# The opening of a fused state-space and feed-forward kernel: C over two queues, decay differences in other banks, the first top words copied by GpSimd

## The chip, the cores and the metric

The kernel runs on one core of one Trainium2 chip. The metric is the device time of one execution in microseconds; the median of the runs of a kernel counts. Each core has a matrix engine (TensorE, PE), a vector engine (VectorE, DVE), a scalar engine (ScalarE, ACT), GpSimd (POOL) and SyncE (SP), which here only issues transfers. Transfers can be issued from SP and from ACT; both share the core's 16 DMA engines.

## What is computed

Shapes: 4 batches, 8 heads, 768 tokens, head size 32, state size 16; feed-forward 256 to 2048 to 256.

```python
log_a = np.log(np.clip(a, 1e-06, 1.0))
for each chunk of 32 tokens:
    cum = np.cumsum(la, axis=-1)
    L = np.exp(cum[:, :, :, None] - cum[:, :, None, :]) * causal
    CB = np.einsum('bhin,bhjn->bhij', Cc, Bc)
    y_intra = np.einsum('bhij,bhjd->bhid', CB * L, xc)
    y_inter = np.einsum('bhin,bhnd->bhid', Cc, state) * np.exp(cum)[..., None]
    y[:, :, sl] = y_intra + y_inter
    state = exp(sum(la)) * state + sum_j(Bc x xc * exp(cum[-1] - cum_j))
# then, with the heads side by side (3072 tokens of 256):
h = x @ w_in
out = (h * np.clip(h + 3.0, 0.0, 6.0) / 6.0) @ w_out
```

The two weight matrices are given as 64-bit floats.

## The kernel before

The 768 tokens are worked in six chunks of 128 for all four batches at once, each as two halves of 64. The order of instructions on each engine is that of the program; nothing is rescheduled.

For a chunk, `diff_mask`, `diff_less` and `diff_pick` build the differences of the summed logarithms in PSUM (chunks 0 and 1), `diff_exp` takes their exponential into `L` on ScalarE, `scores` multiplies C with B (`cb`) and brings x into the state (`into_state`), `multiply` forms `L` times `cb` on VectorE, `mix` forms y (with `from_state`), and `keep` copies y into `yT`, the input of the feed-forward part. For chunk 0 `turn_squares` transposes C on VectorE and `part_heads` spreads it into `cT`; `turn_b` transposes B on TensorE; `first_eto` and `fade` scale C by the decay; `ends` scales B by the decay (`bs`, on GpSimd).

The feed-forward part of chunk 0 runs over f = 0 to 15, blocks of 128 hidden units: `mlp_in` makes two matmuls of 128x512 into one of four PSUM banks (f modulo 4), `ramp` (ScalarE) and `times_ramp` (VectorE) turn them into `gT`. Behind it `first_out` multiplies with `w_out` in four groups. Later chunks use products with fewer multiplications (`lead`, `early`, `middle`, `last`, `out_units`).

The weights come as eight parts of 1 MB (`raw`, three buffers): parts 0 to 3 are quarters of `w_in`, 4 to 7 of `w_out`. `decode(i)` is a generator that turns a part from 64-bit words into 32-bit floats in steps: a copy of the top 16 bits (`ws`, ScalarE), the masks of exponent and sign (VectorE), the upper and the lower words of the significand (`wm`, VectorE), two ScalarE steps on the exponent (`we`), and sign and product (VectorE). `weights(i, n)` takes n steps. In the loop over f, the table `weave` takes one step of parts 2 to 5 at each f.

Transfers, in the program's order: `a` on SP; the first weights and B of chunk 0 on ACT; C of chunk 0 in eight pieces (`pairs_first`), x and the second weights on SP. Every transfer uses one of eight completion slots in turn, and an issue waits until the previous transfer on its slot is complete. The PSUM banks are called f0 to f3, two called o, and y0 and y1. The order of the opening is written out at the end of the program, from `diff_mask` to `load(1)`.

Of the kernel before, what the change touches and what calls it, by code (L numbers as in the profile page):

```python
# [20 lines left out]
def kernel(  # L21
# [63 lines left out]
    def load_bc(c):  # L85
# [10 lines left out]
        def pairs_first(src):  # L96
            t = loads.tile([P, 2, NB, 4, N], FP32, name="pairs", tag="bc")
            for b in range(NB):
                for h in range(2):
                    nc.sync.dma_start(  # L100
                        out=t[:, h, b].rearrange("s a n -> s (a n)"),
                        in_=src[b, h:NH:2, sl, :].rearrange("h (s a) n -> h s (a n)", a=4))
            return t
# [3 lines left out]
        Bs[c] = tokens_first(B, nc.scalar if c == 0 else nc.sync, name="B")  # L107
        if c == 0:
            bcs[c] = [pairs_first(C), Bs[c]]
        elif c < TURN:  # L110
# [17 lines left out]
    def load_w(i, queue=nc.sync):  # L128
# [10 lines left out]
        queue.dma_start(out=dst, in_=src)  # L139
        raws[i] = raw  # L140

    load_w(0, nc.scalar)
    load_bc(0)
    load_x(0)
    load_w(1)
    nc.scalar.preload_act_table_set("natural_log_exp_and_others")
# [40 lines left out]
    def decode(i):  # L187
# [10 lines left out]
        nc.scalar.copy(out=s, in_=top)  # L198

        def significand():  # L200
# [3 lines left out]
            yield  # L204
            nc.vector.scalar_tensor_tensor(
                out=m.bitcast(FP32), in0=lo, scalar=2.0 ** -32, in1=m, op0=ALU.mult,
                op1=ALU.add)
            yield

        parts_m = significand()  # L210
        if i == 0:
            next(parts_m)
            next(parts_m)
        yield
        nc.vector.tensor_scalar(
            out=e, in0=s, scalar1=0x7FF0, scalar2=None, op0=ALU.bitwise_and)
        nc.vector.tensor_scalar(
            out=s, in0=s, scalar1=0x8000, scalar2=None, op0=ALU.bitwise_and)
        next(parts_m, None)
        yield  # L220
        nc.scalar.activation(e.bitcast(BF16), e, AF.Relu, bias=bias_hi, scale=-8.0)
        yield
        nc.scalar.activation(e, e.bitcast(BF16), AF.Relu, bias=bias_lo, scale=-1.0)
        next(parts_m, None)
        if i and i + NRAW < 2 * NP:
            load_w(i + NRAW)
        yield
        nc.vector.tensor_tensor(out=e, in0=e, in1=s, op=ALU.bitwise_or)
        m, e = m.bitcast(FP32), e.bitcast(BF16)
        if i < NP:  # L230
            dst = w_in[:, :, i * FP * P:(i + 1) * FP * P]
# [345 lines left out]
    def mix(c):  # L577
# [5 lines left out]
        for u in range(2):  # L583
# [8 lines left out]
            if c == 0:  # L592
                from_state(c, 1, (2 * u, 2 * u + 1))
# [441 lines left out]
```

## Time and profile before

| | us |
|---|---|
| median of three runs | 360.6 (359.11 to 360.76) |
| the profiled execution, time | 359.64 |
| the profiled execution, span | 357.9 |
| PE busy | 347.9 (97%), 3936 instructions |
| DVE busy | 221.9 (62%), 426 |
| ACT busy | 177.5 (50%), 390 |
| POOL busy | 137.9 (39%), 139 |
| DMA | 24.97 MB in 75482 packets |

A profile shows one execution. Its span runs from the first to the last instruction; the execution's own time lies 1.74 us above it. Busy times are averages over stages with different limits, so that a stage is read from the chain of waits (the work that ended last, followed back) and from the timeline of each engine. "Idle before" names what released an engine. A matmul of 128x512 in 32-bit floats has two records.

### The profile page before, as it was taken

The page shows a single profiled execution, that of the slowest core. Times are in us where ns is not written, and L with a number is a line of the kernel's source. Part 1 is how long each engine was busy: PE and PEld are TensorE (multiplying, and loading weights), DVE is VectorE, ACT ScalarE, POOL GpSimd, SP SyncE. Part 2 cuts the span into 40 slices and gives each one's busy share as a digit, 9 for nine tenths or more (in the row PEclk, how much of TensorE's full clock was granted, in tenths as well). Part 3 has the DMA queues.
Part 4 walks back from the last instruction along what each step waited for, and adds up shares of the span by engine and source line. Part 5 has one row for each costly group of instructions (what it writes and reads, how often), then busy time and mean ns, then how long its engine had stood idle before and what let it go on. Part 6 is the DMA issues. An engine that isn't in the chain of part 4 may idle for free.

```text
span 357.9 us, 9350 instructions
## 1 busy us (share of the span) xinstructions
PE 347.9 (97%) x3936; PEld 300.0 (84%) x3936; DVE 221.9 (62%) x426; ACT 177.5 (50%) x390; POOL 137.9 (39%) x139
## 2 busy tenths in 40 slices
PE   5799999999999999999999999999999999999996
PEld 2554458888888999888999888999888999888996
DVE  6599999975887463686444687434587431588111
ACT  4678887267763730674650575560576010476100
POOL 3300000362599521099522089610068600058700
PEclk9899999999999999999999999999999999999999
DMA  8979969502924061550043560001000000000000
GB/s 166 201 277 185 266 165 127 116 4 84 155 57 60 5 136 58 81 80 2 4 113 82 74 88 2 4 2 35 26 2 1 4 3 31 29 3 0 2 29 31
DMA packets 75482, 24.97 MB, mean 70 GB/s; under 512 B 66032, under 2 KB 71824, under 8 KB 74928
## 3 DMA queue, kind: packets, MB, share of 16 engines
q1 hardware_dynamic: 71056, 23.06, 33.9%
q10 hardware_dynamic: 4384, 1.31, 1.7%
q8 instruction: 31, 0.51, 0.6%
q14 instruction: 11, 0.09, 0.1%
HBM read 21.07 MB, written 3.29 MB: 68 GB/s over the span
## 4 chain that ended last, share of the span: by engine, by line
PE 91%; DVE 3%; DMA 3%; ACT 1%; SPq 1%; issue 0%; DVEq 0%; ACTq 0%
PE ob L766 18%; PE even L652 18%; PE oa L766 18%; PE odd L652 13%; PE o L707 8%; PE h L610 8%; PE y L588 3%; PE y L500 2%; PE cb L522 2%; DMA raw<-in_moe_w_in_dram 2%; DMA pairs<-in_C_dram 1%; PE y L534 1%; SPq L100 1%; DVE odd L681 0%; DVE up L668 0%
## 5 line engine op out<-in xcount | busy, mean ns | idle before, releaser
L752 POOL TENSOR_TENSOR s<-gT 128x512 f32<-128x512 f32 x20 | 26.4, 1318 | 89.7 <-DVE gT L693 89.7
L652 PE MATMUL even<-ts,w_sum 128*128 128x256 f32 x160 | 48.2, 383 | 0.0
L667 ACT COPY even<-odd 128x512 f32<-128x512 f32 x40 | 23.0, 576 | 48.6 <-PE odd L652 46.3
L688 ACT ACTIVATE gT<-odd,half 128x512 f32<-128x512 f32 x40 | 27.5, 688 | 34.9 <-DVE odd L681 34.9
L652 PE MATMUL odd<-yT,w_in 128*128 128x256 f32 x160 | 41.1, 379 | 0.0
L766 PE MATMUL oa<-w_out,gT 128*128 128x128 f32 x320 | 38.9, 277 | 0.0
L766 PEld LDWEIGHTS oa<-w_out,gT 128*128 128x128 f32 x320 | 38.1, 192 | 0.9
L766 PE MATMUL ob<-w_out,s 128*128 128x128 f32 x320 | 37.4, 275 | 0.0
L766 PEld LDWEIGHTS ob<-w_out,s 128*128 128x128 f32 x320 | 36.5, 192 | 0.0
L652 PEld LDWEIGHTS even<-ts,w_sum 128*128 128x128 f32 x160 | 29.9, 190 | 5.3 <-ACT up L674 1.5
L693 DVE SCALAR_TENSOR_TENSOR gT<-gT,odd 128x512 f32<-128x512 f32 x40 | 27.5, 688 | 9.9 <-ACT gT L688 9.9
L652 PEld LDWEIGHTS odd<-yT,w_in 128*128 128x128 f32 x160 | 30.1, 190 | 3.9
L385 ACT ACTIVATE L<-L,cum_n 128x64 f32<-128x64 f32 x128 | 31.1, 339 | 0.0
L766 PE MATMUL ob<-t,gT 128*128 128x128 f32 x240 | 30.3, 279 | 0.0
L688 ACT ACTIVATE gT<-even,half 128x512 f32<-128x512 f32 x40 | 27.8, 695 | 4.4 <-PE even L652 4.4
L693 DVE SCALAR_TENSOR_TENSOR gT<-gT,even 128x512 f32<-128x512 f32 x40 | 27.2, 680 | 4.4 <-ACT gT L688 4.4
L766 PEld LDWEIGHTS ob<-t,gT 128*128 128x128 f32 x240 | 27.9, 192 | 1.2 <-issue 0.5
L707 PE MATMUL o<-w_out,gT 128*128 128x256 f32 x128 | 28.7, 381 | 0.0
L668 DVE COPY up<-odd 128x256 f32<-128x256 f32 x40 | 17.0, 424 | 18.6 <-ACT even L667 17.9
L610 PE MATMUL h<-yT,w_in 128*128 128x512 f32 x64 | 27.7, 594 | 0.0
L707 PEld LDWEIGHTS o<-w_out,gT 128*128 128x128 f32 x128 | 24.1, 190 | 3.7 <-issue 0.5
L563 DVE TENSOR_TENSOR L<-L,cb 128x512 f32<-128x512 f32 x24 | 15.3, 681 | 18.0 <-PE cb L522 15.5
(130 smaller groups left out, 609.8 us busy)
## 6 DMA issues: line engine op xcount, KB each, us to landing
raw<-in_moe_w_out_dram SPq DMA_DIRECT2D x4, 1024.0 KB
L<-cum_d SPq DMA_DIRECT2D x8, 512.0 KB
xt<-in_x_dram SPq DMA_DIRECT2D x6, 512.0 KB
raw<-in_moe_w_in_dram SPq DMA_DIRECT2D x3, 1024.0 KB
out_dram<-res SPq DMA_DIRECT2D x20, 128.0 KB
eto<-cum_e SPq DMA_DIRECT2D x20, 64.0 KB
B<-in_B_dram SPq DMA_DIRECT2D x5, 256.0 KB
raw<-in_moe_w_in_dram ACTq DMA_DIRECT2D x1, 1024.0 KB
```

Of the source, the lines that this page charges most:

```text
L385: nc.scalar.activation(Ls[c][:, b, h], Ls[c][:, b, h], AF.Exp, bias=cum_n[:, c, g:g + 1])
L563: nc.vector.tensor_tensor(out=Ls[c][:, :, hs], in0=Ls[c][:, :, hs], in1=cbs[c][q], op=ALU.mult)
L588: nc.tensor.matmul(out=ys[c][a, u][d0:d0 + D, b], lhsT=xt[rows, b * NH + h], rhs=Ls[c][rows, b, h], start=(b == 0 and a >= min(c, 1)), sto ...
L610: nc.tensor.matmul(out=h.rearrange("p r i -> p (r i)"), lhsT=w_in[:, j, f * P:(f + 1) * P], rhs=yTs[k][:, j].rearrange("p b i -> p (b i)") ...
L652: nc.tensor.matmul(out=bank[:, r], lhsT=lhsT, rhs=rhs, start=start, stop=True, skip_group_check=True)
L667: nc.scalar.copy(out=even, in_=odd[:, 1:2].to_broadcast([P, 2, 2 * P]))
L668: nc.vector.tensor_copy(out=up[:, 1], in_=odd[:, 0])
L688: nc.scalar.activation(gTs[k][:, f], h.rearrange("p r i -> p (r i)"), AF.Relu, bias=half, scale=1.0 / 6.0)
L693: nc.vector.scalar_tensor_tensor(out=g, in0=g, scalar=1.0, in1=h.rearrange("p r i -> p (r i)"), op0=ALU.min, op1=ALU.mult)
L707: nc.tensor.matmul(out=o[:, b % 2], lhsT=gTs[0][:, f, b * P:(b + 1) * P], rhs=w_out[:, f], start=(f == 0 and b % 2 == 0), stop=True, skip_ ...
L752: nc.gpsimd.tensor_tensor(out=o, in0=p_, in1=q_, op=op)
L766: nc.tensor.matmul(out=bank[:, slot], lhsT=lhs[:, j], rhs=rhs[:, j], start=(clear and j == 0), stop=True, skip_group_check=True)
```

## The change

C of chunk 0 is loaded in pieces of 32 partitions with all four batches, in place of 128 partitions and one batch, alternately from ACT and SP. The first weights move from ACT to SP, behind C; B follows them on SP, then x, and the second weights in four pieces. ScalarE's table load now stands ahead of its transfers.

The differences of chunk 0 use the banks o and y0, y1 in place of f0 to f3. Those of chunk 1 are split: the masks and `diff_less` of batches 0 and 1 stay in the opening, their `diff_pick` goes to f = 3, all of batches 2 and 3 to f = 5, and the exponentials of batches 2 and 3 into `first_out`.

For part 0 the top words are copied by GpSimd, and the lower words, sign and product stand behind the decay products. For part 1 all steps stand behind `keep`. The loads of parts 2 and 3, formerly issued ahead of and behind `scores`, are issued from ACT behind the first step of part 1 and from SP behind f = 0; `load_eto(1)` and `load(1)` go to f = 1. `turn_cum` moves into the middle of `mix(0)`, the filler matmul `busy` ahead of it is gone, and one copy of `in_three` goes to ScalarE.

```diff
-        def pairs_first(src):
+        def pairs_first(src, queues=(nc.sync, nc.sync)):
             t = loads.tile([P, 2, NB, 4, N], FP32, name="pairs", tag="bc")
-            for b in range(NB):
+            for q in range(NQ):
                 for h in range(2):
-                    nc.sync.dma_start(
-                        out=t[:, h, b].rearrange("s a n -> s (a n)"),
-                        in_=src[b, h:NH:2, sl, :].rearrange("h (s a) n -> h s (a n)", a=4))
+                    queues[h].dma_start(
+                        out=t[32 * q:32 * q + 32, h].rearrange("s b a n -> s b (a n)"),
+                        in_=src[:, 2 * q + h, sl, :].rearrange("b (s a) n -> s b (a n)", a=4))
...
-        Bs[c] = tokens_first(B, nc.scalar if c == 0 else nc.sync, name="B")
         if c == 0:
-            bcs[c] = [pairs_first(C), Bs[c]]
-        elif c < TURN:
+            bcs[c] = [pairs_first(C, (nc.scalar, nc.sync))]
+            load_w(0)
+        Bs[c] = tokens_first(B, name="B")
+        if c < TURN:
...
-        queue.dma_start(out=dst, in_=src)
+        for r in range(n):
+            rows = slice(r * P // n, (r + 1) * P // n)
+            queue.dma_start(out=dst[rows], in_=src[rows])
...
-    load_w(0, nc.scalar)
+    nc.scalar.preload_act_table_set("natural_log_exp_and_others")
     load_bc(0)
     load_x(0)
-    load_w(1)
-    nc.scalar.preload_act_table_set("natural_log_exp_and_others")
+    load_w(1, n=4)
...
+        def words():
+            if i == 0:
+                nc.gpsimd.tensor_copy(out=s, in_=top)
+            else:
+                nc.scalar.copy(out=s, in_=top)
...
+        def more():
+            if i + NRAW < 2 * NP:
+                load_w(i + NRAW)
...
+        order = {
+            0: ((words,), (upper,), (masks,), (above,), (below,), (lower,), (sign, product),
+                (more,)),
+            1: ((words,), (upper,), (masks, above), (lower, below), (sign, product), (more,)),
+        }.get(i, ((words,), (masks, upper), (above,), (below, lower, more), (sign, product)))
...
-        nc.vector.tensor_copy(part[G:2 * G], mid)
+        nc.scalar.copy(out=part[G:2 * G], in_=mid)
...
-        if c == 0:
-            d = ps.tile([P, NH, HT], FP32, name="d", tag=f"f{b}")
-        elif b < 2:
+        if b < 2:
...
-        take(c)
+        if c:
+            take(c)
...
+            if then is not None and u == 0:
+                then()
...
     diff(0, 0, 1)
     diff(0, 2, 3)
+    turn_squares(bcs[0][0], turned(0)[2])
+    part_heads(0)
     weights(0, 1)
+    weights(0, 1)
+    add_up(ends_at[1])
+    store_rows()
     for b in range(NB):
         diff_exp(0, b)
+        ends(0, b)
+    for b in range(2):
+        diff_mask(1, b)
+    turn_b(0)
     first_eto()
-    diff(1, 2, 3)
...
+    for b in range(2):
+        diff_less(1, b)
     fade(0, HALF[1], nc.gpsimd)
...
-    load_w(2)
+    weights(0, 2)
     weights(0, 1)
     scores(0)
     multiply(0)
-    load_w(3)
-    c_ps = ps.tile([P, NC, G], FP32, name="c_ps", tag="f1")
-    turn_cum(c_ps)
-    busy(1, ps.tile([P, NB * P], FP32, name="d", tag="f0"))
-    weights(0, 1)
+    weights(0, 2)
+    c_ps = ps.tile([P, NC, G], FP32, name="c_ps", tag="f2")
+    mix(0, lambda: turn_cum(c_ps))
+    by_token(c_ps)
+    keep(0)
     weights(1, 1)
-    by_token(c_ps)
-    mix(0)
-    keep(0)
-    weights(1, 3)
+    load_w(2, nc.scalar)
+    weights(1, 4)
     renew(0)
-    weights(1, 1)
-    load_eto(1)
-    load(1)
...
                 mlp_in(k, f)
+                if f == 0:
+                    weights(0, 1)
                 for i in weave.get(f, []):
                     weights(i, 1)
-                if f in (6, 8):
+                if f == 1:
+                    load_eto(c)
+                    load(c)
+                elif f == 2:
+                    weights(1, 1)
+                elif f == 3:
+                    for b in range(2):
+                        diff_pick(c, b)
+                elif f == 5:
+                    diff_two(c, 2, 3)
+                elif f in (6, 8):
                     diff_exp(c, f // 2 - 3)
...
+                    elif (i, b) in ((0, 1), (0, 2)):
+                        diff_exp(c, b + 1)
```

## The prediction

> **What bounds the kernel now.** I read the busy table of the page first (TensorE 97% of the span), then the chain of waits in order of time, because a busy share cannot say where an opening is bound.
>
> ```profile
> 0.80 5.83 DMA raw<-in_moe_w_in_dram
> 7.31 1.21 SPq L100
> 8.56 4.29 DMA pairs<-in_C_dram
> 13.03 1.10 DVE csT L465
> 15.19 2.12 PE cb L522 x64
> 17.31 1.30 DVE L L563 x2
> 19.08 1.05 PE d L490 x2
> ...
> 23.36 27.66 PE h L610 x64
> 51.02 15.54 PE o L707 x72
> ```
>
> Columns are start, length, what. Up to 23.3 us the chain is a chain of latencies. Transfers share eight completion slots; the sixth C transfer takes the slot of the first weights (`raw`), so SP waits until `raw` has landed (7.31), C is complete only at 12.85, and everything follows: transpose, `cb`, decay products, `mix`. From 23.3 us on TensorE never waits: 64 records of `h` at 0.433 each, then `o`. So the time is (start of the first `h`, called M, now 23.29) plus all TensorE work behind it plus its stalls. An instruction put behind M costs its full TensorE time, unless TensorE stands still there.
>
> Next the table by short stretches (length, busy time with counts of PE, PEld, DVE, ACT, POOL, then granted clock, DMA share, GB/s):
>
> ```profile
> 6.00:6.50 0.50, 0.00 (x0) 0.00 (x0) 0.47 (x2) 0.00 (x0) 0.00 (x0) 1.00 1.52 167
> 8.00:8.50 0.50, 0.50 (x33) 0.50 (x32) 0.47 (x2) 0.04 (x1) 0.00 (x0) 1.00 0.37 41
> 15.50:16.00 0.50, 0.50 (x32) 0.50 (x27) 0.50 (x1) 0.00 (x0) 0.50 (x1) 0.50 1.02 336
> 20.50:21.00 0.50, 0.50 (x54) 0.41 (x31) 0.50 (x1) 0.00 (x0) 0.00 (x0) 1.00 1.05 426
> ```
>
> The 64-byte pieces of B move at 167 GB/s, the late C pieces at 41, weights at about 400; and `cb` runs at clock 0.50. Last, the timeline of VectorE and ScalarE around M:
>
> ```profile
> 20.43 1.23 DVE L236 SCALAR_TENSOR_TENSOR w_in<-wm,we 128x1024 f32<-128x1024 f32 x1
> 26.48 1.13 ACT L198 COPY ws<-raw 128x1024 uint16<-128x1024 uint16 x1
> 26.77 1.23 DVE L236 SCALAR_TENSOR_TENSOR w_in<-wm,we 128x1024 f32<-128x1024 f32 x1
> 34.37 1.23 DVE L236 SCALAR_TENSOR_TENSOR w_in<-wm,we 128x1024 f32<-128x1024 f32 x1
> ```
>
> Quarter 0 of `w_in` is ready at 21.7, quarter 1 at 28.0 (needed at M + 6.9 = 30.2), quarter 2 at 35.6 (needed 37.2): the weight decoding runs only 1.6 us ahead.
>
> **Two rules of the Trainium skill.** "DMA: Bandwidth & Descriptors", in the section on why a DMA increments its semaphore by 16, says that a transfer from SP or ACT runs on the largest number of engines up to 16 that divides the slowest dimension of both sides. Old C transfers have 4 heads against 128 partitions, hence 4 engines; the DMA share of 0.37 at 41 GB/s while they were alone fits roughly. New ones have 32 and 32, hence 16. I go by it: C's eight pieces stop being slow. "TensorE: Matmul & The Clock Gate", Part 1, says that about 3.4 us of idleness halves the clock and as much work restores it. The trace halves it at about 15.1 after only 2.4 us without matmuls and restores it at about 18.4; I go by the trace, and keep `cb` at its half-speed 2.1 us.
>
> **The change part by part.** Order of issue: SP has `a`, four C, then `raw` 0, B, x, `raw` 1 in four pieces; ACT has its table load and four C. On SP the first four C issues ended at 4.2 in the old run; the next, `raw` 0, needs the slot of the first C (about 1.27 + 3.1, the 3.1 being `a`'s issue to landing: 4.4). Weights issued at 17.05 began to flow at about 18.6, so +1.5: 5.9. Then 1.05 MB at 400 GB/s is 2.65: 8.6. B lies behind it in the same queue: 262 KB at 165 GB/s, 1.6: 10.2. From end of flow to first use was 0.9 for the old `raw` 0 (5.75 to 6.66): B usable at 11.1. C needs nothing of this: its last piece on ACT waits for `a` (3.9) and lands near 7 to 7.5, and transpose and the two `cT` (2.0 in all) are over near 10. Thus B replaces C as the opening's last input.
>
> From B: PE transposes and the ACT copy to `bT` took 11.05 to 12.33, so `cb` starts at 12.4, against 15.19. To the first decay product 2.12 (14.55), four of them 2.4 (16.95). The lower words now stand behind them: 1.14, sign 0.72, product 1.2: quarter 0 ready at 20.05. TensorE would be ready sooner: `mix` needs two decay products (15.8), took 3.2, and has the 0.43 of `turn_cum` inside it: 19.5. The removed filler (1.05) stood ahead of `mix`, so TensorE loses it as a cause of delay. M = 20.1: **gain 3.2 us**.
>
> Hidden edits. GpSimd's copy of the top words has no row; the nearest is its 512-element copy, 1.01, so 2.0 for 1024, and 2.6 by its tensor-tensor (1.32 for 512). It delays the four `bs` (1.53) and `fade` (1.5) queued behind it: 9.5 + 2.0 = 11.5, `bs` until 13.0, `fade` until 14.6, needed at 14.5 (the decay product overwrites what `bs` reads) and 16.8. Cover 1.5 us; a copy of over 3.5 us would put its excess on the path, and no copy can gain more than that slack. VectorE's `upper` waits for `raw` 0 (9.5) with the second scan and the masks queued behind it: 0.6 + 1.2 + 0.9 end at 12.2, covered until the first decay product (14.55); the stores of rows that SP holds for that scan are read only for chunk 1. One split copy moved to ACT: +0.1 of hops, in C's shadow. Ln on ACT slips by about 0.4 behind the last C issue: same shadow. The x transfer (3.0 to 3.4 of flow behind B) lands at 14.4 against 14.5 needed: exposed only if a gap opens between the two, up to 2 us as between C and B of chunk 1.
>
> What is put behind M. Chunk 1's decay differences, formerly in idle TensorE time, are now between `h` instructions. From the timeline: 32 picks 0.62 (7.98 to 8.60), two `less` with the wait for picks 0.54, two masks 0.43 at full clock. At f = 3: 0.62. At f = 5: 0.43 + 0.54 + 0.62 = 1.6. **Loss 2.2 us.** The other two `less` stay ahead of M. Bounds: 1.7 (no drain between shapes) to 2.8.
>
> The third weights. Their load was issued at 17.05 and idle long before its copy at 26.48; now ACT issues it behind the copy of the top words of part 1, at M to M + 1.1, say 20.6 (whether the issue waits for the copy the trace does not show: both ends kept). With 1.5 + 2.65 + 0.9 it lands at 25.7 if alone. It is not: SP's `raw` 3 (issued about 18.3, flowing 19.9 to 22.6) and then the chunk-1 rows, C and B, moved ahead to f = 1, share the engines; halving its rate throughout gives 28.3. Its copy stands in ACT's order ahead of `ramp` of f = 1; the bank of f = 1 is wanted again by f = 5 at M + 9.3 = 29.4. From landing to bank free: copy 1.04, `ramp` 0.67, VectorE's `times_ramp` 0.65, so it must land by 27.0. I take 27.5: **loss 0.5 us**, range 0 to 1.3 (below nothing: no, the bank cannot be early for a TensorE that does not wait). Quarter 1: top words copied by 21.2, masks to 22.2, above and below to 24.5, sign and product 26.4, needed 27.6; safe.
>
> C and B of chunk 1, `raw` 4 to 7, the two exponentials put at the first `o` groups: ACT has gaps of 0.4 to 1.0 there, and SP's `raw` 4, even behind all small pieces, would land near 35 against about 38. Nothing.
>
> Sum on the profiled execution (span 357.9, with 1.74 around it 359.64): -3.2 + 2.2 + 0.5 = -0.5, so 359.1. That execution lies 1.0 below the median of the three runs shown (360.6); on the median: 360.1 us. About 0.5%, 1.8 us, is what a measurement of this kernel can tell from no change.
>
> **Rivals.**
> (1) The weights come in time and TensorE is warm at `cb` (1.0 instead of 2.1), or the added matmuls partly fill stalls: -3.2 - 1.1 + 2.0 = -2.3, 358.3 us. For: the gap ahead of `cb` is now broken up by masks, transposes and `e_ps`. Against: 2.4 us of idleness was enough before. Chance 0.22.
> (2) The third weights get a third of the engines beside `raw` 3, the four rows, C and B, because the small pieces hold an engine for 1.5 times their share (share 1.5 to 1.7 in the old stretches of small pieces). 1.05 MB then takes 7.9: flow from 22.1 to 30.0, landing 30.9, 3.9 too late: -3.2 + 2.2 + 3.9 = +2.9, 363.5 us. It decides from a landing of 28.0, where the gain is used up, and by 29.8 it costs 0.5%. For: old `raw` loads never had a second queue of small pieces beside them. Against: pieces of several KB should take more than an even share. Chance 0.18.
> (3) x comes late by the 2 us gap: `into_state` and `mix` wait, M = 21.6, sum +1.0, 361.6 us. For: SP stood 4.66 us in issuing B of chunk 1 behind C. Against: x behind B of chunk 1 flowed without a gap. Chance 0.2.
> (4) The slot wait is not on the path and C would have been late anyhow: excluded by the 7.31 line, at most 0.02.
> My forecast itself: 0.38.
>
> **How the numbers follow.** Forecast 360.1 with its own range of 359.0 to 361.5; rivals at 358.3, 361.6 and 363.5. Eight in ten lie within 358.2 and 363.0: this leaves out the quicker half of (1) and most of (2). Faster by over 0.5%: (1) mostly, 0.2. Slower by over 0.5%: (2) and a corner of (3), 0.22. Within: 0.58.
>
> **What would show it.** Right: C's transpose near 8, `cb` near 12.4, first `h` near 20.1, matmuls of `diff_less` and `diff_pick` between those of `h` summing to 2.2, a short TensorE stall at f = 5 released by VectorE. Wrong: `cb` above 14 (B or x slower), a first `h` above 21.5, GpSimd's copy over 3.5 us, the third top-words copy on ACT idle until after 28, or a TensorE clock below 1.00 during `mix`.

## The result, and the profile after

The changed kernel takes 364.04 us (median of 4 runs, 364.01 to 365.24) against 360.52 (359.11 to 360.76) for the kernel before on the same chip: 1.0114 times as long, 95% interval 1.0081 to 1.0147. That is slower by more than the 0.5% that a measurement of this kernel can tell from no change, and 1.0 us above the top of the predicted eight-in-ten range. The profiled execution took 364.05 us with a span of 362.2 (before: 359.64 and 357.9), so 4.3 us of span are to be explained.

Most of a line number's change is mere shift: `h` is now L629, `mix` L605, `into_state` L549, `from_state` L513, `diff_pick` L370, `diff_less` L361, the masks L349, `o` L726. First the chain of waits in order of time (start, length, what).

```profile
4.51 12.08 DMA xt<-in_x_dram
16.60 0.14 issue
16.73 0.89 PE y L549 x49
17.62 0.61 ACT mid L574 x2
...
18.54 0.86 PE y L605 x53
...
20.37 0.65 PE y L605 x45
21.02 1.50 issue
22.52 0.34 PE y L605 x15
...
23.47 8.76 PE h L629 x16
32.23 0.62 PE d L370 x32
32.86 3.63 PE h L629 x8
36.49 0.43 PE d L349 x2
36.92 0.43 PE d L361 x2
37.35 0.62 PE d L370 x32
37.98 17.36 PE h L629 x40
55.34 4.75 PE o L726 x22
```

Three things stand here that the old chain did not have. The opening is now bound by x (landed 16.6), not by C. In the middle of `mix`, at 21.02, TensorE stands still for 1.50 us and nothing that the profile knows of released it ("issue"). And behind M the first 16 records of `h`, which the forecast put at 6.93 us, took 8.76. The sum from these rows, against the old `o` at 51.02:

- first `h` of the chain 23.36 to 23.47: +0.11 (the forecast had -3.2)
- f = 0 to 3, 8.76 instead of 16 x 0.433 = 6.93: +1.83
- chunk 1's differences, 0.62 + 0.43 + 0.43 + 0.62: +2.10
- f = 4 and 5, 3.63 instead of 8 x 0.433 = 3.46: +0.17

Together 4.2 of the 4.32 us by which `o` starts later. This is the sum of one execution. The four executions show a mean granted clock of 0.981, 0.991, 0.995 (the profiled one) and 1.000, and took 365.24, 364.01, 364.05 and 364.03 us: the one without any half clock was no faster, so the 1.83 us are not a cost that can simply be taken off. Now the short stretches (length, busy time with counts of PE, PEld, DVE, ACT, POOL, then granted clock, DMA share, GB/s), the same as were shown of before and two new ones:

```profile
6.00:6.50 0.50, 0.00 (x0) 0.00 (x0) 0.45 (x2) 0.40 (x1) 0.00 (x0) 1.00 0.82 319
8.00:8.50 0.50, 0.50 (x23) 0.46 (x18) 0.47 (x2) 0.30 (x1) 0.00 (x0) 1.00 1.29 182
15.50:16.00 0.50, 0.00 (x0) 0.00 (x0) 0.50 (x2) 0.50 (x1) 0.00 (x0) 1.00 1.01 188
20.50:21.00 0.50, 0.50 (x49) 0.38 (x32) 0.50 (x2) 0.00 (x0) 0.00 (x0) 1.00 0.76 145
21.50:22.00 0.50, 0.00 (x0) 0.00 (x0) 0.50 (x1) 0.00 (x0) 0.00 (x0) 1.00 0.86 336
24.50:25.00 0.50, 0.50 (x2) 0.31 (x1) 0.07 (x1) 0.40 (x1) 0.00 (x0) 0.50 0.40 117
```

The crawl at 41 GB/s behind C is gone (in 8.00 the first weights' end and B's pieces move at 182), but TensorE stands idle in 15.50 and again in 21.50, and its half clock has moved: before it lay at 15.1 to 18.5, in `cb`, ahead of M; now it lies at 24.0 to 27.4, inside `h`, where every microsecond counts. Last the timeline rows of SP, GpSimd, VectorE, ScalarE and TensorE that answer to the steps of the forecast (the bracket is the idle time before, and what ended it):

```profile
4.51 5.48 SPq L119 DMA_DIRECT2D xt<-in_x_dram  x1
6.47 1.08 DVE L478 STREAM_TRANSPOSE csT<-pairs 128x512 f32<-128x512 f32 x1
9.52 1.63 POOL L203 COPY ws<-raw 128x1024 uint16<-128x1024 uint16 x1 [4.44 <-DMA raw<-in_moe_w_in_dram]
10.10 2.12 DVE L284 TENSOR_TENSOR_SCAN pre<-pre 32x512 f32<-32x512 f32 x1
19.60 1.23 DVE L244 SCALAR_TENSOR_TENSOR w_in<-wm,we 128x1024 f32<-128x1024 f32 x1
31.51 1.11 ACT L205 COPY ws<-raw 128x1024 uint16<-128x1024 uint16 x1 [3.21 <-DMA raw<-in_moe_w_in_dram]
39.11 1.23 DVE L244 SCALAR_TENSOR_TENSOR w_in<-wm,we 128x1024 f32<-128x1024 f32 x1
16.73 0.85 PE L549 MATMUL y<-xt,bs 64*32 64x64 f32 x64 [1.45 <-DMA xt<-in_x_dram]
```

C did what was forecast: its transpose starts at 6.47 instead of 13.03. Weight quarter 2 was ready at 40.3 instead of 35.6.

B and x can be told apart by the size of their pieces, 64 and 128 bytes. These are the packet counts of the changed kernel in 8.50:10.00, 10.20:10.80 and 11.00:14.00:

```profile
DMA packets 3021, 0.20 MB, mean 134 GB/s; under 512 B 3019, under 2 KB 3019, under 8 KB 3021
DMA packets 189, 0.02 MB, mean 29 GB/s; under 512 B 189, under 2 KB 189, under 8 KB 189
DMA packets 3548, 0.45 MB, mean 151 GB/s; under 512 B 3548, under 2 KB 3548, under 8 KB 3548
```

66 bytes a packet first, 127 in the last: B flowed first and x behind it. Packet by packet, B's pieces run from 7.9 to 10.9 us, thinning out from 10.0 on, and x's from 10.7 to 14.9. TensorE could use B at 12.46 and x at 16.73, so 1.6 and 1.8 us passed between the last packet and the first use.

### The profile page after: what moved, and what is told of

It is laid out like the page before. It is cut to its first block, busy times and chain, and to the rows that moved or that the text cites. A ratio compares the mean times of both kernels' runs of the same rounds, so it can differ in the third digit from the quotient of the medians.

```text
span 362.2 us, 9360 instructions
## 1 busy us (share of the span) xinstructions
PE 350.1 (97%) x3936; PEld 300.0 (83%) x3936; DVE 223.9 (62%) x425; ACT 176.7 (49%) x390; POOL 139.9 (39%) x140
## 4 chain that ended last, share of the span: by engine, by line
PE 90%; DMA 4%; DVE 2%; ACT 1%; issue 1%; SPq 0%; DVEq 0%; ACTq 0%
PE ob L785 18%; PE even L671 18%; PE oa L785 17%; PE odd L671 13%; PE h L629 8%; PE o L726 8%; DMA xt<-in_x_dram 3%; PE y L605 3%; PE y L513 2%; PE cb L535 1%; PE y L549 1%; DMA pairs<-in_C_dram 1%; DVE odd L700 0%; DVE up L687 0%; ACT even L686 0%
## 5 line engine op out<-in xcount | busy, mean ns | idle before, releaser
L707 ACT ACTIVATE gT<-odd,half 128x512 f32<-128x512 f32 x40 | 27.5, 687 | 34.9 <-DVE odd L700 34.9
L712 DVE SCALAR_TENSOR_TENSOR gT<-gT,odd 128x512 f32<-128x512 f32 x40 | 27.5, 688 | 9.9 <-ACT gT L707 9.9
L629 PE MATMUL h<-yT,w_in 128*128 128x512 f32 x64 | 30.0, 626 | 0.0
L726 PE MATMUL o<-w_out,gT 128*128 128x256 f32 x128 | 28.7, 381 | 0.0
L687 DVE COPY up<-odd 128x256 f32<-128x256 f32 x40 | 17.0, 425 | 18.6 <-ACT even L686 17.9
L416 POOL TENSOR_TENSOR tmp<-state,eto 128x256 f32<-128x256 f32 x5 | 3.3, 652 | 64.9 <-DMA eto<-cum_e 57.6
L726 PEld LDWEIGHTS o<-w_out,gT 128*128 128x128 f32 x128 | 24.1, 190 | 3.7 <-issue 0.4
```

What stands on the lines that cost most here:

```text
L629: nc.tensor.matmul(out=h.rearrange("p r i -> p (r i)"), lhsT=w_in[:, j, f * P:(f + 1) * P], rhs=yTs[k][:, j].rearrange("p b i -> p (b i)") ...
L687: nc.vector.tensor_copy(out=up[:, 1], in_=odd[:, 0])
L707: nc.scalar.activation(gTs[k][:, f], h.rearrange("p r i -> p (r i)"), AF.Relu, bias=half, scale=1.0 / 6.0)
L712: nc.vector.scalar_tensor_tensor(out=g, in0=g, scalar=1.0, in1=h.rearrange("p r i -> p (r i)"), op0=ALU.min, op1=ALU.mult)
L726: nc.tensor.matmul(out=o[:, b % 2], lhsT=gTs[0][:, f, b * P:(b + 1) * P], rhs=w_out[:, f], start=(f == 0 and b % 2 == 0), stop=True, skip_ ...
```

## What stops TensorE: reading the pause

The page counts transfers that no line of the kernel issues:

```profile
q8 instruction: 31, 0.51, 0.6%
```

31 packets of 16.4 KB. TensorE executes 3936 pairs of weight load and matmul, and 3936 / 128 = 30.75: one packet for every 128 pairs. Counting the pairs in order of time puts the 1.50 us pause at pair 349. In every run of this study, an "issue" pause of more than a quarter of a microsecond inside the opening fell at pair 220 to 222, 348 to 351 or 476 to 480, whichever instruction stood there. So TensorE works through blocks of 128 pairs, and where a block's instructions are not there, it stops. The times of the packets fit. In all kernels together TensorE has 25 gaps of more than a quarter of a microsecond without a releaser, here and in later stages (none of them in the kernel before or in e11); each ended 1.2 to 1.6 us after the end of such a packet, and 2.2 to 3.0 us after its start. That this is the supply of TensorE's instructions is therefore shown by the place and by the time of the stops. In the table, the packet of the next block begins 0.6 to 4.3 us after TensorE's entry into a block; the entry as executed is only near the moment of the request, for one boundary earlier, at pair 94, the same distance runs from -0.4 us (e6) to 3.2 (e7). The table has the block from pair 222 to 350. In the kernel before it holds `into_state` and the first half of `mix` with what stands between them; in the changed kernel, which has 66 fewer pairs ahead of `cb`, it is nearly all `mix`.

| kernel | enters pair 222 at | packet, start to end | passes pair 350 at | stop there |
|---|---|---|---|---|
| before | 17.16 | 18.18 to 19.14 | 20.81 | none |
| after | 18.59 | 20.02 to 21.05 | 22.52 | 1.50 |
| e3 | 17.96 | 19.94 to 20.96 | 22.36 | 1.54 |
| e4 | 16.01 | 17.60 to 19.21 | 20.56 | 1.42 |
| e5 | 18.45 | 19.66 to 20.68 | 22.13 | 1.04 |
| e6 | 16.47 | 20.14 to 21.18 | 22.52 | 3.40 |
| e7 | 19.57 | 23.83 to 24.82 | 26.41 | 3.47 |
| e8 | 16.57 | 20.52 to 21.49 | 22.93 | 3.37 |
| e9 | 17.29 | 18.05 to 19.29 | 20.68 | 0.93 |
| e10 | 16.23 | 17.43 to 18.34 | 19.68 | 0.33 |
| e11 | 16.32 | 16.94 to 17.87 | 21.30 | none |
| e12 | 16.31 | 17.44 to 18.82 | 20.31 | 0.88 |

(e1 had its stop, 1.06 us, one boundary earlier, at 21.13; e2, with other instructions in front, one later, 0.96 us at 25.32. At pair 222 itself e4, e7, e8, e10 and e12 stopped too, for 0.55 to 0.82 us. In e5 the pair ahead of 222 ran 1.2 us earlier, before a wait for x, so that its entry is uncertain by that.) The kernel before spends 3.65 us on these 128 pairs, because the block has the filler `busy` (1.05 us), the transposes of the cumulative sums, a wait of 0.34 us and `into_state` at half clock in it; the next block has arrived by then. The changed kernel has no filler and a full clock and is through after 2.4 us of work. It meets a deadline that the old one did not know of.

## The experiments

Twelve kernels ran. Letters in the texts on record stand for the theory that each text names; "Q" is in the first group the order of the transfers of B and x, in the last group the queue in which the instruction packet waits.

**e1: B on ScalarE's queue.** In the changed kernel:

```
-        Bs[c] = tokens_first(B, name="B")
+        Bs[c] = tokens_first(B, nc.scalar if c == 0 else nc.sync, name="B")
```

> The changed kernel with B of chunk 0 on ACT's queue behind C, so that x stands directly behind the first weights on SP. Theory Q (x came late because its pieces queue behind B's 4096 pieces on SP): x lands near 12 to 13 instead of 16.6, `into_state` follows `cb` without a wait, `mix` starts about 1.5 us earlier, the first `h` near 21 to 22; time 361 to 362.5 us against 364.0. Rival (the pause of TensorE in `mix` and the half clock are set by other things and take the gain back): the first `h` stays within 0.5 of 23.4, 363.5 to 364.5 us.

368.80 us, 1.0238 (1.0215 to 1.0261) of before. From its chain of waits:

```profile
3.56 11.69 DMA B<-in_B_dram
15.30 1.11 PE t_ps L435 x4
```

And from its DMA queues in 9.00:13.00 (packets, MB; q1 is SP, q10 ScalarE):

```profile
q1 hardware_dynamic: 2736, 0.35, 93.6%
q10 hardware_dynamic: 2732, 0.17, 78.1%
```

TensorE no longer waited for x, but for B, which landed at 15.25, where the changed kernel could use it at 12.46: in two queues the pieces of 64 and of 128 bytes went one for one, so that B, the smaller, took until 13.8, and x still until 14.4. The expected 12 to 13 for x was missed. What the two need together did not shrink. `cb` waited until 17.41, the half clock lay at 11.8 to 18.6 and 22.0 to 32.2, first `h` at 27.16.

**e2: dummy matmuls ahead of B's transposes**, to move what stands at the pause:

```
+    for _ in range(56):
+        nc.tensor.matmul(
+            out=ds[1, 0][0:32, 0], lhsT=ident[0:64, 0:32], rhs=ident[0:64, 0:64], start=True,
+            stop=True, tile_position=(0, 0), skip_group_check=True)
+    mask_again(1, 0)
```

> The changed kernel with 56 small added matmuls ahead of the transposes of B, into a bank that a mask overwrites; nothing else is moved. Theory F (the 1.5 us pause in the second half of `mix` is TensorE waiting for its next block of instructions, and struck there because fewer instructions now lie ahead of it): the pause leaves `mix`, first `h` near 22, and if TensorE's clock then stays at 1.00 about 1.7 us more are saved in the first four f: 360.5 to 362.5 us. Rival (the pause belongs to `mix` itself or to the load on the DMA engines at 20 to 22 us): a pause of about 1.5 us at the same matmul, 364 us or slightly more for the added work.

372.61 us, 1.035 (1.0321 to 1.0378). They took 6.4 us, far more than planned, so the time says nothing about the 360.5 to 362.5 expected. The place does: the old position in `mix` ran without a stop, and TensorE stopped 0.96 us in `from_state` instead, at 25.32, again 128 pairs on. Each of these matmuls counts as two pairs in the profile. This is the run that ties the stop to the count and not to an instruction.

**e3: the differences back ahead of M.**

```
+        elif c:
+            d = ps.tile([P, NH, HT], FP32, name="d", tag=f"f{b}")
...
-    for b in range(2):
+    for b in range(NB):
         diff_mask(1, b)
...
+    diff(1, 2, 3)
+    for b in (2, 3):
+        diff_exp(1, b)
...
-    scores(0)
+    scores(0, lambda: [diff_pick(1, b) for b in range(2)])
...
-                elif f == 3:
-                    for b in range(2):
-                        diff_pick(c, b)
-                elif f == 5:
-                    diff_two(c, 2, 3)
```

> The changed kernel with all of chunk 1's differences back ahead of the first `h`: batches 2 and 3 in the banks f2 and f3 behind those of chunk 0, the picks of batches 0 and 1 between `cb` and `into_state`, where TensorE waits for x. Theory D (behind M they cost their full TensorE time, 2.1 us): at least 2.1 less, 361.9 us. If theory F holds too, 64 more small matmuls lie ahead of `mix` and the 1.5 us pause is gone or moved, and with less idleness the clock holds: down to 358.5 us. Rival (stalls behind M would have taken their place, e.g. by the third weights, which land at 31.4): 363 us or more.

364.18 us, 1.0102 (1.0069 to 1.0134): no better than the changed kernel with 2.10 us of TensorE work taken out from behind M. First `h` at 24.94, the pause unchanged, and then a new bound (chain of waits):

```profile
25.22 6.70 DMA raw<-in_moe_w_in_dram
...
31.94 1.14 ACT ws L205
...
33.69 0.69 DVE gT L714
...
37.20 1.14 DVE wm L219
...
39.57 1.23 DVE w_in L244
```

Of the 2.10 us, 1.5 were lost ahead of M: TensorE waited for x until 17.73 here. The rest went behind it. The third weights land at 31.9, and from there the chain is VectorE's and ScalarE's decoding, not TensorE; `h` stood idle for 0.44 us at f = 8 and 0.36 at f = 12, both ended by VectorE's `w_in`. In the changed kernel the late load had cost 0.17 us at most, covered by the other losses; take these away and it sets the pace.

**e4: the kernel before with C's new pieces and nothing else.**

```
-            for b in range(NB):
+            for q in range(NQ):
                 for h in range(2):
...
-                        out=t[:, h, b].rearrange("s a n -> s (a n)"),
-                        in_=src[b, h:NH:2, sl, :].rearrange("h (s a) n -> h s (a n)", a=4))
+                        out=t[32 * q:32 * q + 32, h].rearrange("s b a n -> s b (a n)"),
+                        in_=src[:, 2 * q + h, sl, :].rearrange("b (s a) n -> s b (a n)", a=4))
```

> The kernel before with only the new shape of C's pieces (32 partitions, all four batches), all on SP. Theory K (old pieces ran on 4 engines, new ones on 16): the pieces move at over 100 GB/s, the last lands near 11.3 instead of 12.85, `cb` up to 1.5 us earlier, 359.0 to 360.0 us. Rival (the wait for the slot of the first weights sets the end, the shape does not matter): 360.5 us.

364.15 us (10 runs, 361.32 to 365.55), 1.0099 (1.0063 to 1.0135); the profiled execution took 362.27. Its chain of waits:

```profile
7.64 4.04 DMA pairs<-in_C_dram
...
14.04 1.20 PE cb L522 x60
...
15.46 0.55 issue
...
19.14 1.42 issue
...
23.30 30.51 PE h L610 x64
```

This is the cleanest run of the study: one part alone, a part that works (C lands at 11.69 instead of 12.85, `cb` starts at 14.04 instead of 15.19 and runs at full clock), and the kernel is slower than the 359.0 to 360.0 expected and than before. The 1.15 us of gain, and the 0.9 of a warm `cb`, are lost in two stops of 0.55 and 1.42, so that `h` starts where it did. The clock then falls to half from 22.2 to 29.0, and `h` takes 30.51 instead of 27.66. None of its ten executions has a mean clock above 0.995; of the 13 of the kernel before beside them, five have 1.000.

**e5: e3 with two more masks and the two `less` between `cb` and `into_state`.**

```
-    for b in range(2):
-        diff_less(1, b)
...
-    scores(0, lambda: [diff_pick(1, b) for b in range(2)])
+    scores(0, lambda: [part(1, b) for part in (mask_again, diff_less, diff_pick)
+                       for b in range(2)])
```

> e3 with two more small instruction pairs (masks) between `cb` and `into_state`, and `diff_less` of batches 0 and 1 moved there too. Theory F2: TensorE gets its instructions in blocks of 128 pairs of load and matmul; in all runs so far it paused at pairs 221, 349 or 479 of its count, and the next block is there about 4 us after it enters one. e3 stood just ahead of pair 221 while it waited for x; here it enters that block before the wait, at about 16.2, so that the next is there by about 20.5: no pause in `mix` (or under 0.4), first `h` 23.4 to 23.7 against 24.9 in e3. Rival (the pause comes from the transfers in flight at 20 to 22 us, not from the count): a pause of about 1.5 us stays. The time itself may stay near 363 us, because the third weights still land at about 31.5.

365.45 us, 1.0134 (1.0096 to 1.0172). Under 0.4 was expected; TensorE stopped 1.04 us at the same pair, 0.5 less than in e3. The clock was at half for 10.2 us from 21.6 on.

**e6: e5 with the third weights issued before `scores`**, on SP instead of ScalarE.

```
+    load_w(2)
...
-    load_w(2, nc.scalar)
```

> e5 with the third weights issued on SP ahead of `scores`, as in the kernel before. Theory W (in e3 the third weights, landing at 31.9, made VectorE's decoding the bound and ate the 2.1 us of the differences): they land by 24, no ScalarE wait for them, the `h` phase takes 27.7 to 28.5 us; 359 to 361 us. Rival (VectorE's decoding is late for other reasons, e.g. all of part 1 behind `keep`): 362.5 us or more.

365.91 us, 1.0153 (1.011 to 1.0196), where 359 to 361 was expected. The third weights came in time, but TensorE stopped for 3.40 us. That refuted the rule that the runs so far had suggested, that a block simply comes 4 us after the entry into the one before: here TensorE had entered at 16.47 and got its instructions at 22.52. The packet itself began late (20.1).

**e7: the changed kernel with TensorE kept busy** by six masks in the wait for x and four masks and `less` ahead of `mix`.

```
-    for b in range(2):
-        diff_less(1, b)
...
-    scores(0)
+    scores(0, lambda: [mask_again(1, b) for _ in range(3) for b in range(2)])
     multiply(0)
+    for b in (0, 1, 0, 1):
+        mask_again(1, b)
+    for b in range(2):
+        diff_less(1, b)
```

> The changed kernel with TensorE kept busy in two waits: six masks while it waits for x, four masks and the two `diff_less` ahead of `mix` (banks that are written afresh behind them). Theory C (idleness from 15.3 to 22.5 halves the clock at 24.0 to 27.3, in the bound `h` phase, and costs 1.7 us): if the filled waits are enough, clock 1.00 throughout, first four f in 6.9 instead of 8.8 us, but then the stall for the third weights (landing 31.4) shows: 362.5 to 363.5 us. Rival (the 1.5 us pause alone is enough to halve the clock): clock 0.50 stays for 3 us or more, 364 us.

368.51 us, 1.0234 (1.0185 to 1.0283). The remedy for the clock made the stop 3.47 us long (22.94 to 26.41) and the clock fell all the same (13.6 to 17.0 and 27.3 to 30.7). So it is not less work in the block alone that makes a stop: the packet began later.

**e8: e4 with 64 small matmuls ahead of `cb`.**

```
+    for i in range(64):
+        nc.tensor.matmul(
+            out=pad_ps[HALF[i % 2], i % NH], lhsT=pick[:, :1].to_broadcast([P, HT]),
+            rhs=split[:, 0, HALF[0]], start=True, stop=True,
+            tile_position=(0, (i % 2) * HT), skip_group_check=True)
```

> e4 (the kernel before with the new shape of C) with 64 small matmuls ahead of `cb`, into the bank f2 that `cb` then overwrites; nothing else moved. Theory F2: pair 222 is entered at the start of `cb`, pair 350 by the end of `into_state` more than 4 us later, so neither of e4's pauses (0.55 and 1.42) is left, TensorE stays at clock 1.00 through `mix` and `h`: first `h` at 21 to 21.5, h phase 27.7 us, 358 to 359 us, faster than both kernels. Rival (the gain of C only moves the wait elsewhere): first `h` 23 or later, 360 to 364 us as e4.

368.29 us (365.92 to 370.91), 1.0211 (1.0167 to 1.0255), where 358 to 359 was expected. In the profiled execution, at 370.91 the upper end of the six, TensorE stopped 0.78 us at pair 222 and 3.37 at pair 350.

The last three have something in common: the packet began 3.7 to 4.3 us after TensorE's entry, where it was 1.6 in e4 and 1.4 in the changed kernel. In e7 and e8 a weight transfer of 1 MB had been issued 0.3 and 0.6 us before the entry (19.29 against 19.57; 15.94 against 16.57), and 1 MB takes some 2.5 us. But one was issued 0.1 us before it in the kernel before (17.05) and in e4 (15.90) too, and there the packet began after 1.0 and 1.6. The next group takes such transfers away.

**e9: the changed kernel with the weights held back.**

```
-    load_w(1, n=4)
...
             nc.scalar.copy(out=dst, in_=y)
+            if c == 0 and a == u == 0:
+                load_w(1, nc.scalar)
...
-            0: ((words,), (upper,), (masks,), (above,), (below,), (lower,), (sign, product),
-                (more,)),
+            0: ((words,), (upper,), (masks,), (above,), (below,), (lower,), (sign, product)),
...
     load_w(2, nc.scalar)
+    load_w(3, nc.scalar)
```

> The changed kernel with the loads of the second, third and fourth weights issued on ScalarE's queue only after the first yT copy (second) and after the second weights' top words (third and fourth), so that hardly any weight traffic is queued between 16.6 and 20 us. Theory Q (TensorE asks for the block of instructions after next when it enters a block; that fetch stands in its DMA engine behind the weight transfers queued before it, 1.4 us in the changed kernel, and is usable some 2.5 us after it begins): TensorE enters its block at 18.6 as before, the fetch begins by 18.9 instead of 20.0, the pause at 21.0 falls from 1.50 to 0.4 us or less, the first h stands at 22.0 to 22.4 instead of 23.47, and if the shorter pause also leaves the clock at 1.00 the first four f take 6.9 instead of 8.76; time 361 to 362.5. Rival P (the fetch has a pace of its own that no load changes): fetch at 20.0, pause 1.5 us, first h 23.4, time 364 within 1. A third outcome, a gain in the pause that is lost to a later second or third weight, would show as a wait of h on VectorE at f=4 or f=8.

365.37 us, 1.0129 (1.0086 to 1.0172). The stretch ahead of the packet's start, in the table by short stretches (the last two columns are DMA share and GB/s):

```profile
17.50:18.00 0.50, 0.50 (x61) 0.48 (x37) 0.50 (x1) 0.00 (x0) 0.00 (x0) 1.00 0.00 0
```

And from its chain of waits:

```profile
18.15 5.65 DMA raw<-in_moe_w_in_dram
...
29.68 1.22 DVE w_in L243
...
32.54 3.70 PE h L629 x8
```

With nothing on the DMA engines the packet began 0.8 us after the entry instead of 1.4, and the stop was 0.93 instead of 1.50; x came sooner too (used at 15.43 instead of 16.73), first `h` stood at 21.6, and f = 0 to 3 ran at full clock in the profiled execution, at 363.88 the lower end of the six and the only one of them with a mean clock of 1.000. So the load is part of it. The expected 0.4 was missed: here a block takes 0.8 to the packet and 2.6 to its use, 3.4 us, and the work in it is 2.4. The whole gain, and more, was then lost by the third outcome named: the held-back second weights made `h` wait 3.2 us for VectorE at f = 4.

**e10: e4 with the weights held back.**

```
     load_x(0)
-    load_w(1)
...
         take(c)
+        if c == 0:
+            load_w(1, nc.scalar)
...
-    load_w(2)
     weights(0, 1)
     scores(0)
     multiply(0)
-    load_w(3)
...
-    weights(1, 1)
     by_token(c_ps)
     mix(0)
     keep(0)
+    weights(1, 1)
+    load_w(2, nc.scalar)
+    load_w(3, nc.scalar)
```

> The kernel before with C's pieces in the new shape (as in the run that lost its gain to two pauses of TensorE, 364.15) and with the loads of the second to fourth weights held back in the same way, the second on ScalarE behind the copy of adds, the third and fourth behind the second's top words, these words copied after the yT copies. Theory Q: the block after entry 222 at 15.5 to 16.0 is fetched at once, by 16.3 instead of 17.5, usable by 18.9, so the pause of 1.42 us inside mix is gone or under 0.2; first h 21.3 to 22.0 instead of 23.30; with the clock at 1.00 through the first h stage the time is 358 to 359.5, under the kernel before. Rival P: pause of 1.4 us again, first h 23.3, half clock for some us in the h stage, 363 to 365.

360.92 us (22 runs), 1.0022 (1.0006 to 1.0039): level with before within the 0.5% that can be told here, where e4 was at 1.0099 and 358 to 359.5 was expected. In the profiled execution, at 360.14 the lower end of the 22, the stop at pair 350 was 0.33 instead of 1.42 (the one at pair 222 stayed, 0.64), first `h` at 21.92, 1.4 us ahead of before, and the clock never fell. The packet began only 0.2 us sooner than in e4, but it took 0.92 us where e4's took 1.61. The rest again went to the decoding: the second weights' words came late, `h` waited 0.65 us at f = 4, and VectorE carries the chain from there to 62 us. The clock does not hide a gain: with a mean clock of 1.000 thirteen executions of e10 have a median of 360.8, and twelve of the kernel before, on the same chip, 359.6.

**e11: the kernel before with the same holding back**, as control (the same edit without C's pieces).

> The kernel before with nothing but the same holding back of the second to fourth weights: the control for what the holding itself costs. Theory Q: no pause of TensorE in the opening (there was none to remove), first h 23.3 as before or up to 0.2 later for the DMA issue on ScalarE ahead of mid; time 360.5 within 1. Rival (the later weights become the bound): a wait of h on VectorE or a DMA at f=4 or f=8, and 361.5 to 363.

362.81 us (11 runs, 361.26 to 363.87), 1.0058 (1.0033 to 1.0082). No stop, but this stretch:

```profile
16.25:20.00 3.75, 3.46 (x78) 1.94 (x70) 3.55 (x6) 1.00 (x3) 0.41 (x1) 0.50 0.55 122
```

The clock, which in the profile of the kernel before is at half for 3.41 us after the idle stretch ahead of `cb`, stayed there for 13.65 us (16.25 to 29.90), so that `mix` came late and `h` took 30.21. Neither theory had named this. The time lies in the rival's 361.5 to 363, but without the wait on VectorE that it named. And this execution, at 363.87, is the upper end of the eleven: the mean clock of the others runs from 0.98 to 1.000, and the kernel before has executions at 0.98 too, six of the 83 measured beside these runs, at 363.5 to 364.0 us. The long half clock is thus not a consequence of the holding alone, and a comparison of this profile with e10's, which is the lower end of its kernel, would say too much about C's pieces.

**e12: e10 with the loads staggered** and the second weights' lower words worked out first.

```
-        if i == 0:
+        if i < 2:
             next(parts_m)
...
             nc.scalar.copy(out=dst, in_=y)
+            if c == 0 and a == u == 0:
+                load_w(2, nc.scalar)
...
-    load_w(2, nc.scalar)
     load_w(3, nc.scalar)
```

> The run with C's new pieces and the loads held back (first h at 21.92 instead of 23.29, but 360.92 us: the second weights' lower words were worked out only behind their top words, VectorE idle from 19.95 to 23.44), with two edits: VectorE works out the second weights' lower words as soon as they have landed (about 21.7), ahead of their top words, and the third weights are issued behind the first yT copy (19.8) instead of at 22.3. Theory Q with the bound handed to VectorE: first h again at 21.9, pauses as there (0.3 to 0.6 us), the second weights ready 1 us sooner so that h does not wait at f=4, the 1.4 us kept to the end: 358.8 to 359.8. Rival (VectorE's decoding bounds the rest of the h stage in any case, or the earlier third load brings the longer pause back): the h stage waits on VectorE again and the time is 360.5 to 361.5.

360.50 us (22 runs), 1.0012 (0.9989 to 1.0035): no difference from before. The stops grew to 0.82 and 0.88 (first `h` 22.55) and the bound stayed with VectorE; its chain of waits:

```profile
17.18 5.20 DMA raw<-in_moe_w_in_dram
...
23.14 1.23 DVE wm L204
...
27.10 0.70 DVE we L227
...
42.93 1.23 DVE w_in L235
```

The rival was right. No version tried beats the kernel before: with M earlier by 0.7 (e12) and 1.4 us (e10), the decoding of the weights takes TensorE's place as the bound of the first `h` stage.

## Why the prediction was wrong

The step that failed is the one that put M at 20.1. M was 23.47 on the chain, 3.4 us later: 1.9 because the times for B and x were too short, and 1.5 because TensorE waited for its own instructions in the middle of `mix`, which the sum did not have. In the profiled execution a half clock behind M, put at nothing as well, added 1.8.

**C: right.** The slowest dimension of 32 instead of 4 takes the piece from the rule of four engines to sixteen, as "DMA: Bandwidth & Descriptors" of the Trainium skill says in its section on why a DMA increments its semaphore by 16. No trace here shows the number of engines; what they show agrees. In the changed kernel C is long done; in e4, with the old order of issue, SP's issue of a piece took 0.44 us (median) instead of 0.72, and C lands at 11.69 instead of 12.85, of which 0.9 is the earlier issue of the last piece (7.64 instead of 8.56).

**B and x: wrong by 1.4 and 2.2 us.** The step "B lies behind it in the same queue: 262 KB at 165 GB/s, 1.6: 10.2" rests on a misreading. The 167 GB/s of the stretch 6.00:6.50 were not B's alone; by queue that stretch of the kernel before is (B came on q10, C on q1):

```profile
q10 hardware_dynamic: 973, 0.06, 133.8%
q1 hardware_dynamic: 82, 0.02, 18.4%
```

B's 973 packets of 64 bytes in half a microsecond are 124 GB/s. In the changed kernel its pieces took 3.0 us (7.9 to 10.9) instead of 1.6, and 1.6 instead of 0.9 passed to the first use: usable at 12.46, forecast 11.1. x lay behind it, as the forecast had it, and no gap of 2 us opened (rival (3)); but its flow took 4.2 us instead of 3.0 to 3.4, and it was used at 16.73 instead of 14.5. e9 splits this lateness: with the second weights held back x was used at 15.43, so 1.3 us of it go with the second weights, which flow beside x's end. TensorE waited 1.45 us for x. The half clock in `cb` did not come (1.21 instead of 2.1), which gave back 0.9.

**The filler and `mix`: costed as pure gain, wrong by 1.5 us.** "The removed filler (1.05) stood ahead of `mix`, so TensorE loses it as a cause of delay" put the filler's removal at a gain, and `mix` was costed at its old 3.2 us with the 0.43 of `turn_cum`. `mix` took 4.9, of which 1.50 was the wait for the next block of instructions. That the filler had covered this wait in the kernel before is argued from the table: it is 1.05 of the 3.65 us that the block lasts there. No run puts the filler alone back. e4, which keeps it, shows that it is not enough by itself: there a warm and earlier opening is through the block's work in 3.1 us. e7, which puts other work in its place, shows a longer stop.

**The clock.** The forecast let it fall ahead of M or not at all; it named a clock below 1.00 during `mix`, but not behind M. In the profile it fell 1.5 us after the pause ended, and `h` took 1.83 us more. "TensorE: Matmul & The Clock Gate", Part 1, describes a free-running window of about 3.4 us. The trace agrees on the window: every half-clock stretch of the study lasts 3.41 us or 2, 3 or 4 times that. That stops bring it on is supported by e4 and e10, which differ in the loads held back and in the stop, 1.42 us in one profile and 0.33 in the other: mean clock 1.000 in none of ten executions of e4 and in 13 of 22 of e10. The changed kernel and e9 do not support it: 1.000 in one of four and in one of six, though the stop was 1.50 and 0.93 in the profiles. So this cause is likely, not shown. And no threshold follows: in e5 stops of 0.97, 0.96 and 1.04 within 4.7 us went with 10.24 us at half, while the changed kernel's own wait of 1.45 us for x, at 15.3, was followed by none. Nor does TensorE's busy share in a whole window of 3.41 us decide: 0.70 was followed by half clock in e2, 0.46 by none in e9. The length of the half clock differs between executions of one kernel, too, and the runs do not show what ends it.

Why the execution with a full clock was no faster is not shown. The third weights may be the reason. The bank that f = 5 needs came free at 33.9, and f = 5 began at 34.6; with `h` 1.83 us sooner it would have waited 1.1 of these (an estimate from the changed kernel's rows).

**The differences behind M: right.** Forecast 2.2, measured 2.10, with the parts at 0.62 and 0.43 + 0.43 + 0.62.

**The third weights: mechanism right, size hidden.** Forecast to land at 27.5 and to cost 0.5; landed at 31.5, later than rival (2) had it (30.9). The issue came at 23.69 instead of 20.6, because M was late, and from issue to landing it took 7.8 us instead of 6.9; the fourth weights had come through by 24, before its own pieces began at 25, but from 28 on B of chunk 1 ran beside it. It cost 0.17 at most, because the first `h` (+3.4 us) and the half clock (+1.8 us) had put off the moment at which its bank is wanted by 5.2 us. In e3, with part of that cover gone, `h` stood idle for 0.8 us behind it.

**GpSimd's copy: right** (1.63 for a forecast 2.0, bound 2.6), and off the path.

On the profiled execution the sum was 359.1 and became 364.05. The miss of 4.95 is 1.9 (B and x, with the 0.9 of the warm `cb` already taken off) + 1.5 (pause) + 1.8 (clock) - 0.1 (differences) - 0.3 (third weights) = 4.8. These are the parts of one execution; they overlap, as the clock and the third weights do.

## What to carry to other kernels

A stretch of many small matmuls can have a supply limit of its own: count the pairs of weight load and matmul between two points, and if 128 of them take less than about 3.5 us (the block took 3.4 in e9, with the DMA engines empty), look for "issue" pauses every 128 pairs before promising a gain from a tighter schedule. Filler that looks idle may be what covers this; work put in elsewhere may make it worse, as in e7. Tell streams apart before taking a rate from a stretch: the size of the pieces and the queue say whose bytes they are. Where two engines are level, as TensorE and the decoding on VectorE are here, an earlier start of one is worth only the slack of the other: find that slack before counting the gain (in the kernel before, quarter 3 of `w_in` was ready at 43.1, and f = 12, which needs it, began at 44.0).

## What the runs showed of the hardware

- TensorE's instructions come in packets of 16.4 KB for 128 pairs (31 packets for 3936 pairs). TensorE went on 1.2 to 1.6 us after the end of the packet in each of the 25 stops. With the DMA engines empty the packet began 0.8 us after entry into a block and could be used 2.6 us later (e9).
- The packet began later when there were more transfers: 0.6 to 1.2 us after entry in the runs with the weights held back (e9 to e12), 1.0 to 4.3 in the others. What decides within this range is open. A weight transfer issued 0.3 to 0.6 us before the entry went with 4.0 and 4.3 (e8, e7), one issued 0.1 us before it with 1.0 and 1.6 (before, e4), one issued 0.2 us behind it with 3.7 (e6). That the packet stands in an engine's queue behind other transfers is not shown.
- In the profiles of the changed kernel, e1, e4 and e5 a stop of TensorE of 1.0 to 1.5 us went with a half clock of 3.41 us or multiples up to 10.24; mean clocks up to 1.000 in other executions of the changed kernel say that it need not. 13.65 us came up in e11, which had no stop.
- Two streams of small pieces share the engines: B ahead of x in one queue was usable at 12.46; in the other queue, piece for piece beside x, it landed at 15.25. The instruction on SP that issues x lasted 5.48 us while B's pieces, issued ahead of it, were flowing, and one that issues B of chunk 1 lasted 7.14.
- VectorE's scan of 32x512 took 2.12 us where a GpSimd copy of 128x1024 words of 16 bits (1.63 us) ran beside its first half, and 1.20 us in the kernel before, beside another GpSimd operation. What lengthened it was not tested.
